# Softmax in three placed steps, reciprocals in PSUM and GpSimd's taps spread, in the first convolution of a fused convolution, Fourier and MLP kernel

## The chip, the cores and the metric

The kernel runs on one core of a Trainium2 chip. The metric is the device time of one execution in microseconds (us), as the median of three runs. Names used throughout: PE is TensorE (matmul), PEld its weight load, DVE is VectorE, ACT is ScalarE, POOL is GpSimd, SP is SyncE, whose queue issues the DMAs. SBUF is the on-chip working memory and PSUM the memory that PE writes its results to; DVE and ACT read and write both.

## The reference

There are 8 batches of 4224 positions by 192 channels, in 8 heads of 24 channels. For each batch:

```python
w = exp(weight_gen - max_k(weight_gen)); w = w / (sum_k(w) + 1e-9)     # softmax over 7 taps, by position and head
y[s, h, g] = sum_k w[s, h, k] * x_pad[s + k, h, g]                     # dynamic causal convolution, 7 taps
u = y + real(fft(fft(y, axis=positions), axis=channels))
un = (u - mean(u)) / sqrt(var(u) + 1e-6)                               # over the 192 channels
out = u + maximum(un @ w_ch1, 0) @ w_ch2                               # 192 -> 768 -> 192
```

## The kernel before

Each batch lies on 128 partitions by 33 rows of 192 channels, with halo rows in front of each half, so that a tap is a shift by one row within a partition. `conv(b)` works in chunks: chunk 8 (`NC`) is row 0 alone, and chunks 0 to 7 have four rows each, two from the lower half and their mirror images.

**Softmax.** `softmax_taps` (L261) is a generator that loads the tap weights of a batch in parts of rows, here (0, 5), (29, 33) and (5, 29), and takes each part in two steps: DMA, maximum (L273), subtraction (L274) and exponential; then sum (L278), L279 and reciprocal (L280). The result of the sum and the reciprocal is the tile `wm`, in SBUF for batch 0 and in a PSUM bank (named `wp` in the trace) for later batches. `tap_step(b, n)` drives the generator up to its n-th step. The normalised weights of a chunk are made by one multiplication (L362, for chunk 8 L365) into the PSUM tile `wp`: weights from SBUF times reciprocals.

**Taps.** For each chunk and tap DVE multiplies rows of `x_sb` by `wp` (L405). `POOL_TAPS` gives some taps of chunks 0, 1 and 3 of batch 0 to POOL, which multiplies by a copy of the weights in SBUF, `wq` (made at L374, product L403). The seven products of a chunk are added in one of two ways. For chunks 0, 1, 3, 5 and 7 of batch 0 (`PE_SUMS`) PE adds them by matmuls with the identity into two banks `pa` (L410; a product is two matmuls, each of which the trace shows as two records), and ACT copies the sum to `u` (L423). For the other chunks POOL adds them one by one (L414); in batch 1 and later DVE takes some of these. Products that PE adds are in tiles of tag `g2` with three buffers; products that POOL adds are in tag `prod` with five. The order of the taps of a chunk that PE adds is POOL's taps first, then the rest:

```python
order = [*pt, *(k for k in range(K) if k not in pt)] if pa else range(K)
```

**Groups.** In batch 0 chunks run in pairs, (8, 0), (1, 2), (3, 4), (5, 6), and then 7 alone, with the taps of a pair interleaved. After a pair come its folds on POOL (`sm`, L428 and L430), the first Fourier matmul (`pg`, L435), two copies on ACT, a sum and a difference on DVE (L444, L446), and the store of `gt` to `g_d` in DRAM. `transform(b)` reads `g_d` back and does the second Fourier step (`pp`, L481), `mix` the one over channels (`eo`, L510), `norm` the normalisation, and `mlp` the two products (`ph` L607, `po` L630).

**Order.** Every engine runs its own queue in order. The framework sets each queue's order when the kernel is built, by its own estimate of when operands are ready, starting from the order in which the code issues the work. The code orders the stages by `add`, `run`, `queue` and `behind`: `conv(0)` alone, then its transform beside the preparation of the MLP weights on DVE (`prep_w1`, `prep_w2`) and the softmax of batch 1, then the MLP of one batch beside the convolution of the next.

Of the kernel before, what the change touches and what calls it, by code (L numbers as in the profile page):

```python
# [38 lines left out]
F32_GROUPS = 7  # L39
WARM = (20, 0, 12, 12)  # L40
# [48 lines left out]
def tile_dynconv_fnet_mlp(  # L89
# [171 lines left out]
    def softmax_taps(b, parts):  # L261

        w_sb = sb.tile([P, N2 * H, K], F32, tag="w_sb", name=f"w_{b}", bufs=2)
        if b == 0:
            m = cpool.tile([P, N2 * H], F32, name=f"wm_{b}")
        else:
            m = wbanks[b][:, 4 * H * K:4 * H * K + N2 * H]
        wv = wg[b].rearrange("p r h k -> p (r h) k")
        for lo, hi in parts:
            sl = slice(lo * H, hi * H)  # L270
            n = (hi - lo) * H
            nc.sync.dma_start(w_sb[:, sl], wv[:, sl])
            nc.vector.tensor_reduce(out=m[:, sl], in_=w_sb[:, sl], axis=AX.X, op=ALU.max)  # L273
            nc.vector.tensor_tensor(out=w_sb[:, sl], in0=w_sb[:, sl],  # L274
                                    in1=m[:, sl].unsqueeze(2).broadcast_to([P, n, K]), op=ALU.subtract)
            nc.scalar.activation(w_sb[:, sl], w_sb[:, sl], AF.Exp)
            yield None
            nc.vector.tensor_reduce(out=m[:, sl], in_=w_sb[:, sl], axis=AX.X, op=ALU.add)  # L278
            nc.vector.tensor_scalar_add(out=m[:, sl], in0=m[:, sl], scalar1=1e-9)  # L279
            nc.vector.reciprocal(out=m[:, sl], in_=m[:, sl])  # L280
            yield w_sb, m
# [3 lines left out]
    def tap_step(b, n):  # L285

        t = taps[b]
        while t["n"] < n:
            t["n"] += 1
            t["tiles"] = next(t["gen"]) or t["tiles"]  # L290

# [4 lines left out]
    def conv(b):  # L296
# [22 lines left out]
        def need_taps(c):  # L319
            nonlocal w_sb, ws  # L320
            while not rows_w.issuperset(rows_of(c)):
                i = next(part_iter)
                rows_w.update(range(*parts[i]))
                tap_step(b, 2 * i + 2)
# [6 lines left out]
        if b == 0:  # L331
            need_x(NC)
            need_x(0)
            need_taps(1)
            need_x(1)
            need_taps(3)
# [3 lines left out]
        gt, tails = None, []  # L340
        for grp in groups:
            chunks = []
            wbank = wbanks[b] if b > 0 else pst("wp", 1, [P, 512], F32, f"wp_{b}_{grp[0]}")
            for i, c in enumerate(grp):
# [27 lines left out]
                elif pt:  # L372
                    wq = sb.tile([P, 2, 2 * H, len(pt)], F32, tag="wq", name=f"wq_{b}_{c}", bufs=2)
                    nc.gpsimd.tensor_tensor(out=wq, in0=win[:, :, :, pt[0]:pt[-1] + 1],  # L374
                                            in1=nin.unsqueeze(3).broadcast_to([P, 2, 2 * H, len(pt)]), op=ALU.mult)
                pa = None
                if on_pe:
                    bank = ("po", 2) if c % 4 == 3 or c == 0 == b else ("ph", 3)
                    pa = [pst(*bank, [P, 512], F32, f"pa_{b}_{c}_{i}") for i in range(2)]
                chunks.append((c, R, u, wp, pa, wq, pt))  # L380
            for i in range(K):
                for c, R, u, wp, pa, wq, pt in chunks:
                    order = [*pt, *(k for k in range(K) if k not in pt)] if pa else range(K)
# [309 lines left out]
    queue(lp, (lambda n: tap_step(1, n), 5))  # L693
# [7 lines left out]
    for g, call in ((1, (prep_w2, 2)), (1, (lambda n: tap_step(1, n), 6))):  # L701
# [82 lines left out]
```

## Time and profile before

| | |
|---|---|
| median of three runs | 1148.77 us (1147.63 to 1149.8) |
| the profiled execution | 1148.59 us, of which its span 1146.8 us |
| PE busy | 1081.0 us, 94% of the span |
| DVE busy | 979.5 us, 85% |
| POOL busy | 877.3 us, 76% |
| ACT busy | 777.8 us, 68% |
| end of the last matmul sum of `conv(0)` | 79.92 us |
| first matmul of the MLP | 125.93 us |

A row of the timeline gives the start from the beginning of the span, the length, the engine, the line and operation, the tile written and those read with their shapes, and the count of like instructions that it stands for. In brackets stand the idle time of the engine before the row and what ended it. Lines are those of the kernel before; the kernel after has the same statements up to ten lines further down. An instruction's length as recorded overlaps a little with the start of the next one on its engine: two multiplications of 128x768 on DVE start 0.87 us apart and are recorded as 0.95 us each.

### The profile page before, as it was taken

To read this page: it belongs to the slowest core of one execution; us is meant where nothing else is said; L and a number is where in the kernel's file an instruction comes from. 1 tells how busy PE (TensorE), PEld (TensorE's weight loads), DVE (VectorE), ACT (ScalarE), POOL (GpSimd) and SP (SyncE) were. 2 spreads that over 40 slices of the span, in tenths; PEclk is the share of its full clock that TensorE was granted. 3 is DMA by queue.
4 is the path that set the end of the run, shared out by engine and by line. 5 is a ranking of instruction groups with operands and counts; after the bars stand their busy time and mean duration, and the time that the engine had idled before them with its cause. 6 is when DMAs were issued, how large, how long until landed. Compare 5 with 4: busy or idle time off the path is not lost.

```text
span 1146.8 us, 23674 instructions
## 1 busy us (share of the span) xinstructions
PE 1081.0 (94%) x8476; PEld 816.4 (71%) x8476; DVE 979.5 (85%) x1825; ACT 777.8 (68%) x2360; POOL 877.3 (76%) x752
## 2 busy tenths in 40 slices
PE   5776799999899999999999999999999999999998
PEld 3345388777577877678777877778768877787777
DVE  7998998889989998999989998999989996356443
ACT  1014677455994689758985699568974898579822
POOL 5959799699996999699969999699969998011200
PEclk9998899999999999999999999999999999999999
DMA  8325244523474147514564238514651133412321
GB/s 301 127 92 155 42 103 106 182 79 80 114 206 128 36 131 196 156 46 113 133 166 110 78 104 212 132 53 118 163 138 56 57 92 92 114 44 59 84 46 46
DMA packets 156502, 128.72 MB, mean 112 GB/s; under 512 B 108571, under 2 KB 133088, under 8 KB 156384
## 3 DMA queue, kind: packets, MB, share of 16 engines
q1 hardware_dynamic: 156384, 127.21, 40.7%
q8 instruction: 67, 1.10, 0.4%
q14 instruction: 51, 0.42, 0.1%
HBM read 61.46 MB, written 39.37 MB: 88 GB/s over the span
## 4 chain that ended last, share of the span: by engine, by line
PE 54%; DVE 15%; POOL 13%; issue 8%; ACT 5%; DMA 4%; SPq 0%; DVEq 0%; POOLq 0%; ACTq 0%
PE ph L607 23%; PE po L630 20%; POOL u L414 10%; DVE pr L405 6%; PE pp L481 3%; PE eo L510 3%; PE pa L410 2%; PE pg L435 2%; DVE hh L618 2%; DMA g<-g_d 2%; POOL hl L574 1%; POOL hl L576 1%; DMA g_d<-gt 1%; ACT un L565 1%; ACT hh L617 1%
## 5 line engine op out<-in xcount | busy, mean ns | idle before, releaser
L414 POOL TENSOR_TENSOR u<-u,pr 128x768 f32<-128x768 f32 (+1 forms) x396 | 657.7, 1687 | 57.1 <-DVE pr L405 44.9
L630 PEld LDWEIGHTS <-hh 128*128 128x128 f16 x4248 | 364.6, 98 | 81.1 <-DVE hh L618 5.2
L630 PE MATMUL po<-w2h,hh 128*128 128x192 f16 x2832 | 415.1, 246 | 5.6 <-DVE hh L618 4.1
L607 PE MATMUL ph<-ht,w1h 128*128 128x512 f16 (+1 forms) x1296 | 395.3, 362 | 6.0 <-DMA ht<-hl 3.2
L405 DVE TENSOR_TENSOR pr<-x_sb,wp 128x768 f32<-128x768 f32 (+1 forms) x420 | 363.2, 888 | 16.6 <-POOL u L414 13.6
L630 PE MATMUL po<-w2l,hh 128*128 128x192 f16 x1416 | 346.4, 246 | 0.0
L618 DVE SCALAR_TENSOR_TENSOR hh<-ph,hh 128x512 f16<-128x512 f32 (+1 forms) x390 | 250.2, 647 | 107.4 <-ACT hh L617 106.6
L607 PE MATMUL ph<-ht,w1l 128*128 128x512 f16 (+1 forms) x864 | 310.4, 362 | 0.0
L617 ACT ACTIVATE hh<-ph 128x512 f16<-128x512 f32 (+1 forms) x390 | 214.1, 551 | 132.4 <-PE ph L607 105.9
L607 PEld LDWEIGHTS <-w1h 128*128 128x128 f16 x1296 | 125.7, 99 | 89.8 <-issue 0.5
L565 ACT ACTIVATE un<-u,rs 128x192 f32<-128x192 f32 x264 | 124.0, 536 | 20.8 <-POOL hl L576 9.6
L574 POOL TENSOR_TENSOR hl<-un,hl 128x512 f16<-128x512 f32 (+1 forms) x69 | 74.9, 1085 | 65.6 <-ACT hl L573 29.3
L607 PEld LDWEIGHTS <-w1l 128*128 128x128 f16 x864 | 85.2, 99 | 54.8 <-issue 7.4
L554 ACT ACTIVATE junk<-u,rs 128x192 f16<-128x192 f32 x244 | 111.0, 455 | 4.1
L550 ACT ACTIVATE junk<-u 128x192 f16<-128x192 f32 x244 | 88.4, 362 | 16.0 <-DVE u L520 13.1
L510 PE MATMUL eo<-cs_sb,pq 97*128 97x97 f32 x544 | 83.1, 276 | 3.7 <-DVE u L520 3.7
L510 PEld LDWEIGHTS eo<-cs_sb,pq 97*128 97x128 f32 x544 | 76.7, 195 | 9.6 <-issue 5.0
L485 ACT COPY pq<-pp 97x204 f32<-97x204 f32 (+1 forms) x96 | 46.9, 489 | 51.5 <-PE pp L481 51.2
L635 DVE SCALAR_TENSOR_TENSOR u<-po,isc,u 128x384 f32<-128x384 f32 (+1 forms) x122 | 74.1, 608 | 6.6 <-PE po L630 6.6
L428 POOL TENSOR_TENSOR sm<-u 128x382 f32<-128x382 f32 x64 | 66.2, 1034 | 9.0 <-ACT u L423 8.7
L410 PE MATMUL pa<-pr,ident 128*128 128x384 f32 x140 | 53.1, 519 | 20.5 <-POOL pr L403 11.3
L630 PE MATMUL po<-w2f,hh 128*128 128x192 f32 x336 | 63.0, 327 | 1.0 <-DVE u L635 1.0
(106 smaller groups left out, 1253.9 us busy)
## 6 DMA issues: line engine op xcount, KB each, us to landing
out_dram<-u SPq DMA_DIRECT2D x64, 384.0 KB
x_sb<-in_x_dram SPq DMA_DIRECT2D x48, 384.0 KB
g<-g_d SPq DMA_DIRECT2D x40, 336.0 KB
x_sb<-in_x_dram SPq DMA_DIRECT2D x8, 864.0 KB
g_d<-gt SPq DMA_DIRECT2D x32, 195.0 KB
g_d<-gt SPq DMA_DIRECT2D x32, 189.0 KB
w<-in_weight_gen_dram SPq DMA_DIRECT2D x6, 924.0 KB
x_sb<-in_x_dram SPq DMA_DIRECT2D x8, 672.0 KB
```

The source lines that it names most:

```text
L405: last_product[b] = nc.vector.tensor_tensor(out=dst, in0=rows, in1=wk, op=ALU.mult)
L410: nc.tensor.matmul(pa[h][:, 0:n], lhsT=ident32, rhs=prf[:, h * n:(h + 1) * n], start=(i == 0), stop=(i == K - 1))
L414: adder.tensor_tensor(out=u, in0=u, in1=pr, op=ALU.add)
L510: nc.tensor.matmul(eo[:, e, j, :], lhsT=pq[0:DH, e, r, r:r + P], rhs=cs_sb[:, e, :], start=True, stop=True)
L550: nc.scalar.activation(junk, uv[:, t, :], AF.Identity, accum_out=st[:, t, 0:1])
L554: nc.scalar.activation(junk, uv[:, t, :], AF.Square, bias=rs[:, 2, t:t + 1], accum_out=st[:, t, 1:2])
L565: nc.scalar.activation(halves[t // 2][:, t % 2, :], uv[:, t, :], AF.Identity, bias=rs[:, 1, t:t + 1], scale=rs[:, 0, t:t + 1])
L574: lo_eng.tensor_tensor(out=hl[:, t0:t1, 2 * P:3 * P], in0=src[:, 0:t1 - t0, 0:P], in1=hl[:, t0:t1, 0:P], op=ALU.subtract)
L607: last_ph[n] = nc.tensor.matmul(ph[:, 0:T], lhsT=wt[:, cs_], rhs=ht[:, 0:T, blk], start=(i == 0), stop=(i == len(terms) - 1))
L617: nc.scalar.activation(a[:, 0:T], ph[:, 0:T], AF.Relu)
L618: nc.vector.scalar_tensor_tensor(out=l[:, 0:T], in0=ph[:, 0:T], scalar=0.0, in1=a[:, 0:T], op0=ALU.max, op1=ALU.subtract)
L630: nc.tensor.matmul(po[t // 2][:, t % 2, :], lhsT=hx[:, t], rhs=wx[:, c2, :], start=(c2 == 0 and i == 0), stop=(c2 == NH - 1 and i == len(t ...
```

## The change

The softmax generator has three steps to a part: DMA; maximum, subtraction and exponential; sum and reciprocal. The callers' counts follow (`3 * i + 3` for `2 * i + 2`; 8 and 9 for 5 and 6), and in batch 0 the DMA of the third part is issued by itself, by `tap_step(0, 7)`, ahead of two pieces of `x`; the rest of that part is issued where chunk 2 first needs it. In batch 0 the third part's maxima, sums and reciprocals lie in a PSUM bank of tag `ph`; those of the first two parts stay in SBUF. Chunk 5 sums into the banks of chunk 1, which leaves that tag its third buffer. `wq` of chunk 3 is made by DVE. The taps of a chunk that PE adds come in the order that `TURNS` spells: `ddpdddd` for one tap of POOL, `dpddpdd` for two, where d is DVE's next tap and p is POOL's.

```diff
--- before.py
+++ after.py
@@ -37,6 +37,7 @@
 POOL_TAPS = {(0, 0): (5, 6), (0, 1): (5, 6), (0, 3): (6,), (1, 0): range(7), (1, 1): range(7)}
 DVE_ADDS = {(1, c): 1 for c in range(2, NC)}
 F32_GROUPS = 7
+TURNS = {1: 'ddpdddd', 2: 'dpddpdd', 3: 'dpddpdp'}
 WARM = (20, 0, 12, 12)
 
 
@@ -261,15 +262,18 @@
     def softmax_taps(b, parts):
 
         w_sb = sb.tile([P, N2 * H, K], F32, tag="w_sb", name=f"w_{b}", bufs=2)
-        if b == 0:
-            m = cpool.tile([P, N2 * H], F32, name=f"wm_{b}")
-        else:
+        if b > 0:
             m = wbanks[b][:, 4 * H * K:4 * H * K + N2 * H]
         wv = wg[b].rearrange("p r h k -> p (r h) k")
         for lo, hi in parts:
             sl = slice(lo * H, hi * H)
+            if b == 0 and lo == 0:
+                m = cpool.tile([P, N2 * H], F32, name=f"wm_{b}")
+            elif b == 0 and hi < N2:
+                m = pst("ph", 3, [P, 512], F32, f"wm_{b}")[:, 0:N2 * H]
             n = (hi - lo) * H
             nc.sync.dma_start(w_sb[:, sl], wv[:, sl])
+            yield None
             nc.vector.tensor_reduce(out=m[:, sl], in_=w_sb[:, sl], axis=AX.X, op=ALU.max)
             nc.vector.tensor_tensor(out=w_sb[:, sl], in0=w_sb[:, sl],
                                     in1=m[:, sl].unsqueeze(2).broadcast_to([P, n, K]), op=ALU.subtract)
@@ -289,6 +293,11 @@
             t["n"] += 1
             t["tiles"] = next(t["gen"]) or t["tiles"]
 
+    def turns(pool, turn):
+
+        its = {"p": iter(pool), "d": (k for k in range(K) if k not in pool)}
+        return [next(its[t]) for t in turn]
+
     def mirrored(ap, step):
 
         return bass.AP(ap.tensor, ap.offset, [ap.ap[0], [step, 2], *ap.ap[1:]])
@@ -321,7 +330,7 @@
             while not rows_w.issuperset(rows_of(c)):
                 i = next(part_iter)
                 rows_w.update(range(*parts[i]))
-                tap_step(b, 2 * i + 2)
+                tap_step(b, 3 * i + 3)
                 w_sb, ws = taps[b]["tiles"]
 
         if b > 0:
@@ -331,13 +340,12 @@
         if b == 0:
             need_x(NC)
             need_x(0)
-            need_taps(1)
+            tap_step(0, 7)
             need_x(1)
-            need_taps(3)
             need_x(3)
             load_consts()
         groups = [(NC, 0), (1, 2), (3, 4), (5, 6), (7,)] if b == 0 else [(c,) for c in range(NC + 1)]
-        gt, tails = None, []
+        gt, tails, sums = None, [], {}
         for grp in groups:
             chunks = []
             wbank = wbanks[b] if b > 0 else pst("wp", 1, [P, 512], F32, f"wp_{b}_{grp[0]}")
@@ -371,16 +379,18 @@
                     wq = win
                 elif pt:
                     wq = sb.tile([P, 2, 2 * H, len(pt)], F32, tag="wq", name=f"wq_{b}_{c}", bufs=2)
-                    nc.gpsimd.tensor_tensor(out=wq, in0=win[:, :, :, pt[0]:pt[-1] + 1],
-                                            in1=nin.unsqueeze(3).broadcast_to([P, 2, 2 * H, len(pt)]), op=ALU.mult)
+                    (nc.vector if c > 1 else nc.gpsimd).tensor_tensor(
+                        out=wq, in0=win[:, :, :, pt[0]:pt[-1] + 1], in1=nin.unsqueeze(3).broadcast_to([P, 2, 2 * H, len(pt)]), op=ALU.mult)
                 pa = None
                 if on_pe:
-                    bank = ("po", 2) if c % 4 == 3 or c == 0 == b else ("ph", 3)
-                    pa = [pst(*bank, [P, 512], F32, f"pa_{b}_{c}_{i}") for i in range(2)]
+                    bank = ("po", 2) if c % 4 == 3 or c == 0 else ("ph", 3)
+                    pa = sums.get(bank)
+                    if pa is None or bank[0] == "po":
+                        pa = sums[bank] = [pst(*bank, [P, 512], F32, f"pa_{b}_{c}_{i}") for i in range(2)]
                 chunks.append((c, R, u, wp, pa, wq, pt))
             for i in range(K):
                 for c, R, u, wp, pa, wq, pt in chunks:
-                    order = [*pt, *(k for k in range(K) if k not in pt)] if pa else range(K)
+                    order = turns(pt, TURNS[len(pt)]) if pt and pa else range(K)
                     k = order[i]
                     pr = u
                     if i > 0 or pa:
@@ -690,7 +700,7 @@
         if at > EARLY / N2:
             break
     queue(lp, (prep_w1, loaded[0]))
-    queue(lp, (lambda n: tap_step(1, n), 5))
+    queue(lp, (lambda n: tap_step(1, n), 8))
     for i in range(2):
         queue(lp, (prep_w2, i))
     for g in range(QUICK):
@@ -698,7 +708,7 @@
         run()
         add(0.0, 1.0, norm(0, g))
         run()
-    for g, call in ((1, (prep_w2, 2)), (1, (lambda n: tap_step(1, n), 6))):
+    for g, call in ((1, (prep_w2, 2)), (1, (lambda n: tap_step(1, n), 9))):
         queue(last_lo[g].ins, call)
 
     def rest():
```

The change moves instructions on the queues of SP, DVE and POOL at the start of batch 0. In the names below, `w_0` are the tap weights of batch 0, `pr_0_c_k` the product of chunk c and tap k, `u_0_c` a chunk's sum, `sm_0_c` its fold, `wp_0_1` the normalised weights of chunks 1 and 2.

SP's queue at the start, before:

```order
L316 DMA x_sb_66<-in_x_dram 128x1344
L316 DMA x_sb_66<-in_x_dram 128x384
L316 DMA x_sb_66<-in_x_dram 128x1728
L316 DMA x_sb_66<-in_x_dram 128x768 x2
L272 DMA w_0_91<-in_weight_gen_dram 128x1344
L316 DMA x_sb_66<-in_x_dram 128x768 x2
```

and now:

```order
L325 DMA x_sb_66<-in_x_dram 128x1344
L325 DMA x_sb_66<-in_x_dram 128x384
L325 DMA x_sb_66<-in_x_dram 128x1728
L275 DMA w_0_91<-in_weight_gen_dram 128x1344
L325 DMA x_sb_66<-in_x_dram 128x768 x4
```

The load of the third part of the weights (128x1344) stood behind two pieces of `x` (128x768) and now stands ahead of them.

DVE's queue in the first pair of chunks, before:

```order
L405 TENSOR_TENSOR u_0_8_133<-x_sb_66,wp_0_8_132 128x192
L405 TENSOR_TENSOR pr_0_8_1_146<-x_sb_66,wp_0_8_132 128x192
L405 TENSOR_TENSOR pr_0_8_2_153<-x_sb_66,wp_0_8_132 128x192
L405 TENSOR_TENSOR pr_0_0_0_156<-x_sb_66,wp_0_8_132 128x768
L405 TENSOR_TENSOR pr_0_8_3_160<-x_sb_66,wp_0_8_132 128x192
L273 TENSOR_REDUCE wm_0_92<-w_0_91 128x192
L405 TENSOR_TENSOR pr_0_0_1_163<-x_sb_66,wp_0_8_132 128x768
L405 TENSOR_TENSOR pr_0_8_4_167<-x_sb_66,wp_0_8_132 128x192
```

and now:

```order
L415 TENSOR_TENSOR u_0_8_128<-x_sb_66,wp_0_8_127 128x192
L415 TENSOR_TENSOR pr_0_0_0_137<-x_sb_66,wp_0_8_127 128x768
L415 TENSOR_TENSOR pr_0_8_1_141<-x_sb_66,wp_0_8_127 128x192
L415 TENSOR_TENSOR pr_0_8_2_148<-x_sb_66,wp_0_8_127 128x192
L415 TENSOR_TENSOR pr_0_0_1_151<-x_sb_66,wp_0_8_127 128x768
L415 TENSOR_TENSOR pr_0_8_3_155<-x_sb_66,wp_0_8_127 128x192
L277 TENSOR_REDUCE wm_0_110<-w_0_91 128x192
L415 TENSOR_TENSOR pr_0_0_2_158<-x_sb_66,wp_0_8_127 128x768
L415 TENSOR_TENSOR pr_0_8_4_162<-x_sb_66,wp_0_8_127 128x192
```

The first product of chunk 0 stands ahead of two small products of chunk 8, and two products of chunk 0 instead of one stand ahead of the maximum over the third part.

POOL's queue behind the additions of chunk 8, before:

```order
L403 TENSOR_TENSOR pr_0_1_5_221<-x_sb_66,wq_0_1_215 128x768
L403 TENSOR_TENSOR pr_0_1_6_226<-x_sb_66,wq_0_1_215 128x768
L374 TENSOR_TENSOR wq_0_3_298<-w_0_91,wm_0_92 128x32
L428 TENSOR_TENSOR sm_0_0_200<-u_0_0_135 128x2x191
L430 TENSOR_TENSOR sm_0_0_200<-u_0_0_135 128x2
L414 TENSOR_TENSOR u_0_2_219<-u_0_2_219,pr_0_2_1_230 128x768
L414 TENSOR_TENSOR u_0_2_219<-u_0_2_219,pr_0_2_2_237 128x768
```

and now:

```order
L438 TENSOR_TENSOR sm_0_0_195<-u_0_0_130 128x2x191
L440 TENSOR_TENSOR sm_0_0_195<-u_0_0_130 128x2
L413 TENSOR_TENSOR pr_0_1_5_227<-x_sb_66,wq_0_1_210 128x768
L424 TENSOR_TENSOR u_0_2_220<-u_0_2_220,pr_0_2_1_231 128x768
L413 TENSOR_TENSOR pr_0_1_6_248<-x_sb_66,wq_0_1_210 128x768
L424 TENSOR_TENSOR u_0_2_220<-u_0_2_220,pr_0_2_2_238 128x768
```

POOL's two products of chunk 1 stood ahead of the fold of chunk 0 and now stand behind it, and an addition of chunk 2 stands between the two. `wq` of chunk 3 has left this queue.

## Rows read from the trace of the kernel before

**Rows 1.** Busy time by stretch of the span, 10 to 76 us.

```profile
core 0: us, PE busy (x) PEld busy (x) DVE busy (x) ACT busy (x) POOL busy (x), PEclk, DMA share, GB/s
...
10.00:16.00 6.00, 4.67 (x8) 2.55 (x9) 3.60 (x6) 0.00 (x0) 3.29 (x3) 1.00 1.02 399
16.00:22.00 6.00, 6.00 (x20) 3.54 (x18) 6.00 (x8) 1.33 (x1) 4.32 (x4) 1.00 0.62 178
22.00:30.00 8.00, 6.66 (x22) 3.50 (x20) 7.97 (x11) 1.64 (x6) 5.23 (x7) 1.00 1.01 358
30.00:40.00 10.00, 7.76 (x22) 3.59 (x22) 9.90 (x13) 0.96 (x2) 9.84 (x8) 1.00 0.46 166
40.00:50.00 10.00, 8.55 (x27) 4.52 (x28) 10.00 (x14) 0.77 (x4) 8.87 (x7) 1.00 0.22 61
50.00:60.00 10.00, 6.82 (x25) 4.06 (x24) 9.88 (x13) 1.72 (x6) 9.06 (x9) 1.00 0.40 129
60.00:70.00 10.00, 7.49 (x21) 3.39 (x20) 9.86 (x16) 0.96 (x2) 9.24 (x6) 1.00 0.25 75
```

**Rows 2.** Timeline of DVE, 0 to 27 us: start, length, what, count, idle before.

```profile
7.38 0.61 DVE L405 TENSOR_TENSOR pr<-x_sb,wp 128x192 f32<-128x192 f32 x2
9.64 1.22 DVE L405 TENSOR_TENSOR pr<-x_sb,wp 128x768 f32<-128x768 f32 x2 [1.65 <-DMA x_sb<-in_x_dram]
13.26 1.55 DVE L273 TENSOR_REDUCE wm<-w 128x192 f32<-128x1344 f32 x1 [2.40 <-DMA w<-in_weight_gen_dram]
...
22.18 1.70 DVE L362 TENSOR_TENSOR wp<-w,wm 128x224 f32<-128x224 f32 x1
23.80 1.34 DVE L280 RECIPROCAL wm<-wm 128x192 f32<-128x192 f32 x1
...
25.83 0.95 DVE L405 TENSOR_TENSOR u<-x_sb,wp 128x768 f32<-128x768 f32 x1
```

**Rows 3.** Timeline of all engines, 0 to 60 us, two of DVE's rows.

```profile
36.85 2.93 DVE L362 TENSOR_TENSOR wp<-w,wm 128x224 f32<-128x224 f32 x2
...
52.11 2.22 DVE L362 TENSOR_TENSOR wp<-w,wm 128x224 f32<-128x224 f32 x2
```

**Rows 4.** Line 362 over the whole span: counts, then duration in ns min/median/max.

```profile
L362 DVE TENSOR_TENSOR wp<-w,wp x54: 385/396/434, 130.9 to 935.8; 128x224 f32<-128x224 f32 x54
L362 DVE TENSOR_TENSOR wp<-w,wm x8: 401/1066/1831, 6.3 to 67.7; 128x224 f32<-128x224 f32 x8
```

**Rows 5.** Timeline of POOL, 0 to 85 us.

```profile
20.64 2.98 POOL L403 TENSOR_TENSOR pr<-x_sb,wq 128x768 f32<-128x768 f32 x2 [0.24 <-PE pa L410]
...
25.64 1.00 POOL L428 TENSOR_TENSOR sm<-u 128x382 f32<-128x382 f32 x1
26.60 0.19 POOL L430 TENSOR_TENSOR sm<-u 128x2 f32<-128x2 f32 x1
27.73 7.50 POOL L414 TENSOR_TENSOR u<-u,pr 128x768 f32<-128x768 f32 x4 [0.93 <-DVE pr L405]
...
36.63 1.80 POOL L414 TENSOR_TENSOR u<-u,pr 128x768 f32<-128x768 f32 x1
...
71.83 0.21 POOL L430 TENSOR_TENSOR sm<-u 128x2 f32<-128x2 f32 x1
```

**Rows 6.** Timeline of PE, 68 to 82 us.

```profile
69.36 4.11 PE L410 MATMUL pa<-pr,ident 128*128 128x384 f32 x12 [0.95 <-DVE pr L405]
...
75.24 0.81 PE L435 MATMUL pg<-sm,f_sb 128*128 128x192 f32 x4
75.89 4.03 PE L410 MATMUL pa<-pr,ident 128*128 128x384 f32 x12
```

**Rows 7.** Timeline of PE, 120 to 132 us, the first product of the MLP.

```profile
125.93 0.38 PE L607 MATMUL ph<-ht,w1h 128*128 128x512 f16 x1
```

**Rows 8.** Busy time by stretch, 200 to 400 us: the sum over the stretches.

```profile
sum 200.00, PE 188.41 PEld 146.41 DVE 184.59 ACT 129.72 POOL 177.90; mean PE 6.28 PEld 4.88 DVE 6.15 ACT 4.32 POOL 5.93
```

**Rows 9.** PE's waits, 130 to 400 us: who for whom, total, times, longest.

```profile
PE po L630 <- DVE hh L618: 3.4, 1, 3.4
```

## Prediction

> **What bounds the kernel now.** The page shows PE busy for most of the span, but the change touches only the first 80 us, before the MLP begins, so I read that part on its own. First the busy time by stretch [rows 1]: from 30 to 70 us DVE is busy 9.86 to 10.0 of every 10 us, POOL 8.87 to 9.84, PE 6.8 to 8.6. So DVE bounds the first convolution, POOL runs close behind, and PE follows. Then DVE's timeline, for what its time is spent on that is not work [rows 2]. It waits 1.65 us for the first large piece of `x`, and 2.40 us, until 13.26, for the third part of the tap weights, which stands in the DMA queue behind two pieces of `x`. From there on it has no wait worth counting until the last chunk. Then the instructions that are longer than they need be: the product that makes the normalised weights, line 362. It takes 1.70 us at 22.18, 2.93 us for two at 36.85 and 2.22 us for two at 52.11 [rows 2, 3], while the same instruction with the reciprocals in PSUM takes 385 to 434 ns in all 54 cases of the later batches, and 401 ns in the best case with both inputs in SBUF [rows 4]. POOL's timeline shows what the long ones lie beside: two products from 20.64 to 23.62, and an addition from 36.63 to 38.43 [rows 5]. As these rows read, a DVE product with both inputs in SBUF stands still while POOL works there.
>
> What follows is a chain. The last matmul sum of this convolution ends at 79.92 (75.89 and 4.03) [rows 6]; fold, transform, mixing and normalisation hang on it, and the first MLP matmul starts at 125.93 [rows 7]. The inputs that come from outside (weights, tables, the next batch) are loaded long before, so I expect a gain at 80 us to arrive at the end.
>
> **The load moved ahead.** The 128x1344 load no longer waits for two pieces of 128x768 in 4 bytes, 786 KB. At the 399 GB/s of the stretch from 10 to 16 us [rows 1] that is 1.97 us, so the weights land at 11.3 instead of 13.26. DVE now starts at 9.64 with a product of chunk 0 (0.87), two small ones (0.27 each; before, they ran at 7.38 in a wait [rows 2]), a second product of chunk 0 (0.87) and a small one (0.27), and reaches the maximum at 12.19. Nothing is left to wait for. Before, the maximum started at 13.26 with that second product still to do: 13.26 + 0.87 - 12.19 = **1.94 us** gained. If the load came no sooner, the maximum would start at 13.26 and 0.87 would be left; that is the lower end.
>
> **Taps spread.** PE now starts after DVE's first product at 10.5 instead of POOL's at 11.3, and gets POOL's products between DVE's. At first a matmul record takes 0.58 us (8 in 4.67), later 0.30 (20 in 6.00) [rows 1], with the same granted clock beside both; four records make a product. PE adds the first three in about 6.5 us, until 17.1. The fourth product of DVE needs the buffer of the third sum, and DVE is ready at 16.54, after the second large softmax instruction: **-0.56 us** (0 to -1). Chunk 0 is complete on PE at about 22.7. POOL's products of chunk 1 now stand behind the fold of chunk 0, so POOL is idle from 19 to about 23.9, and DVE's product for chunk 1, whose reciprocals stay in SBUF, runs without a neighbour at 20.9: 1.62 us from start to next start [rows 2] become 0.42, **1.2 us** (between 0, should POOL run there after all, and 1.3).
>
> **Reciprocals in PSUM.** Chunks 2 to 7 read them from there. The two pairs take 2 x 0.396 instead of 2.93 and 2.22 [rows 3, 4]: 2.14 and 1.43. DVE takes over `wq` of chunk 3, 128x32; I put it at 0.2, the order of the smallest products it does. Together **3.37 us** (2.9 to 3.5). The sums and reciprocals themselves I cost at nothing: DVE's cost does not change with the memory, to judge by line 362 (396 against 401 ns uncontended [rows 4]).
>
> [...]
>
> **Sum on DVE**: 1.94 - 0.56 + 1.2 + 3.37 = 5.95 us by the time DVE starts chunk 7.
>
> **What is late next: POOL.** From the fold of chunk 0, done at about 25.1, POOL has 18 additions at 1.87 (7.50 for four), 3 products at 1.45, and 6 folds at 1.15 (1.00 and 0.19) [rows 5]: 44.9 us, to 70.0, against 72.04 now. PE needs the last of these folds between products of chunk 7. Now it takes it at 75.24 and has three products (12 records, 4.03 us) behind it [rows 6], so POOL has 3.2 us to spare. After the change chunk 7 starts at 63.4 (69.36 less 5.95) and PE wants that fold after five products and one earlier `pg`, at about 70.5, with two products behind it. The slack shrinks to 0.5 us. DVE, POOL and PE then finish almost together, and three queues that tight lose something to each other: **-0.5 us** (0 to -2.5, the last if POOL idles 3 us as it does now, see below). Gain at the end of the convolution: 5.45 us, 3.4 with that last end, 6.7 with all the upper ends; all the lower ends together would leave 0.3.
>
> **Behind it** DVE prepares weights without pause and PE, ACT and DMA follow; all start by the convolution's end, and move with it. The order of the queues differs in places in the MLP of batches 0 and 1 and the start of batch 2, a few instructions swapped with neighbours; I count that as 0, plus or minus 1.
>
> The profiled execution took 1148.59 us, 0.18 below the median of the runs shown. 1148.59 - 5.45 = 1143.1; against the median **1143.3 us**.
>
> **Rivals.**
> *POOL sets the end.* From 30 to 70 us POOL is idle 3.0 of 40 us [rows 1], mostly for DVE's products (0.93 before 27.73 [rows 5]). If it idles as long in the new order it ends at 73.0, three us late, 2.5 more than the slack; the gain is 5.95 - 2.5 = 3.4, the time 1145.3. Against it: DVE runs ahead of POOL by more than before, so there is less to wait for. 14%.
> *The contention stays.* If line 362 is slow for another reason, such as the tile it writes, 3.37 falls away and the gain is 2.1 to 2.6: 1146.4. Against it stand the 54 rows. 4%.
> *The gain is given back.* Between 200 and 400 us PE is idle for 200 - 188.4 = 11.6 us [rows 8]. If those waits hang on something that does not move, such as loads that are paced by buffers, PE waits longer and the gain goes: about 1148, no change. I see no such resource, but 270 us of other work lie between. 12%.
> *Slower: the new order on PE in the MLP of batches 0 and 1.* PE takes its queue in order. Its longest wait there is 3.4 us for DVE's low halves `hh` [rows 9]. Matmuls have changed places by a block of five or ten, and one put ahead of its operand holds all behind it. From 5.45 us more idle time the gain is gone; at 7.8 the kernel is slower by 0.2%. If the idle time doubled the result would be 1143.3 + 11.6 = 1154.9. For it: these queues are set by estimates that the change has shifted. Against: few rows moved, and PE has MLP work either side. 8%.
>
> **Chances.** 0.2% (2.3 us) is about what a measurement of this kernel can tell from no change. The forecast, 1141.8 to 1144.8, has 62%. With the first two rivals the kernel is faster by over 0.2% in 80%, within it in 12%, slower in 8%. The range runs from 1141.5 (a gain of 6.7 and some luck in the order) to 1147.2, which leaves out the slower case, the upper half of the third rival, and little below.
>
> **What would show it.** In the changed profile: the wait before the maximum of the third part under 0.3 us; the products for chunks 2 to 7 near 0.4 us each, the one for chunk 1 too; PE's first sum at about 10.5 and the fold of chunk 0 on POOL at about 24; the last fold of POOL before chunk 7's near 70; the last sum of the convolution ending at 74 to 75 and the first MLP matmul at 120 to 121. The prediction is wrong in its first half if the convolution ends after 77, and in its second if the first MLP matmul comes 5 us sooner and the end does not.

## The result and the profile after

| | before | after |
|---|---|---|
| time, median (us) | 1149.8 (5 runs, 1147.63 to 1154.99) | 1141.5 (5 runs, 1139.6 to 1143.36) |
| profiled execution, span (us) | 1146.8 | 1139.7 |
| last matmul sum of the first convolution ends | 79.92 | 73.88 |
| first MLP matmul starts | 125.93 | 118.64 |

The ratio of the times is 0.9935, 95% interval 0.9915 to 0.9955. The change makes the kernel faster by 0.65%; the forecast was 1143.3 us, with a range of 1141.5 to 1147.2. The measured median thus lies at the lower end of the range, outside the 1141.8 to 1144.8 that had 62%: by the ratio the whole gained 7.5 us, where 5.45 was forecast.

DVE's timeline in the changed kernel, 5 to 72 us, the counterpart of [rows 2, 3] (start, length, what, count, idle before and what ended it; its lines stand 4 to 10 lower than before's):

```profile
9.14 2.61 DVE L415 TENSOR_TENSOR pr<-x_sb,wp 128x768 f32<-128x768 f32 x5 [2.12 <-DMA x_sb<-in_x_dram]
11.67 1.55 DVE L277 TENSOR_REDUCE wm<-w 128x192 f32<-128x1344 f32 x1
...
16.89 1.22 DVE L415 TENSOR_TENSOR pr<-x_sb,wp 128x768 f32<-128x768 f32 x2 [0.76 <-PE pa L420]
...
20.61 0.39 DVE L370 TENSOR_TENSOR wp<-w,wm 128x224 f32<-128x224 f32 x1
20.91 1.36 DVE L284 RECIPROCAL wm<-wm 128x192 f32<-128x192 f32 x1
...
33.99 0.40 DVE L370 TENSOR_TENSOR wp<-w,wm 128x224 f32<-128x224 f32 x1
34.30 0.20 DVE L382 TENSOR_TENSOR wq<-w,wm 128x32 f32<-128x32 f32 x1
34.42 0.40 DVE L370 TENSOR_TENSOR wp<-w,wm 128x224 f32<-128x224 f32 x1
35.41 0.95 DVE L415 TENSOR_TENSOR pr<-x_sb,wp 128x768 f32<-128x768 f32 x1 [0.59 <-DVE wp L370]
...
47.71 0.82 DVE L370 TENSOR_TENSOR wp<-w,wm 128x224 f32<-128x224 f32 x2
...
62.21 3.62 DVE L415 TENSOR_TENSOR pr<-x_sb,wp 128x768 f32<-128x768 f32 x4
```

The maximum of the third part starts at 11.67 without a wait, where it started at 13.26 after 2.40 of waiting. The weight products of chunks 1 to 7 are short. Over the whole span (count, then duration in ns min/median/max), the 54 of later batches and the eight of batch 0, which took 401/1066/1831 before [rows 4]:

```profile
L370 DVE TENSOR_TENSOR wp<-w,wp x54: 369/382/397, 123.9 to 928.8; 128x224 f32<-128x224 f32 x54
L370 DVE TENSOR_TENSOR wp<-w,wm x8: 383/393/400, 6.2 to 61.7; 128x224 f32<-128x224 f32 x8
```

POOL's timeline, 5 to 80 us, the folds of chunk 0 and of the last chunk before 7 [rows 5]:

```profile
22.93 0.99 POOL L438 TENSOR_TENSOR sm<-u 128x382 f32<-128x382 f32 x1 [4.09 <-ACT u L433]
...
67.47 0.99 POOL L438 TENSOR_TENSOR sm<-u 128x382 f32<-128x382 f32 x1
68.42 0.20 POOL L440 TENSOR_TENSOR sm<-u 128x2 f32<-128x2 f32 x1
```

PE's timeline, 5 to 76 us, and further on at the first MLP matmul, where [rows 6, 7] were read:

```profile
10.24 10.47 PE L420 MATMUL pa<-pr,ident 128*128 128x384 f32 x24 [10.24 <-DVE pr L415]
...
63.31 4.11 PE L420 MATMUL pa<-pr,ident 128*128 128x384 f32 x12 [1.29 <-DVE pr L415]
...
70.49 0.81 PE L445 MATMUL pg<-sm,f_sb 128*128 128x192 f32 x4
71.14 2.74 PE L420 MATMUL pa<-pr,ident 128*128 128x384 f32 x8
...
118.64 0.39 PE L617 MATMUL ph<-ht,w1h 128*128 128x512 f16 x1 [0.27 <-DMA ht<-hl]
```

The gain grows along the convolution. The first pair of weight products starts 2.86 us sooner than in [rows 3] (33.99 for 36.85), the second 4.40 (47.71 for 52.11), chunk 7's block of twelve matmul records 6.05 (63.31 for 69.36, [rows 6]), and the last sum ends 6.04 sooner. The first MLP matmul gains 1.25 more, 7.29. On DVE the sum `gt` of chunk 7 stood at 84.08 before and stands at 77.20 now, 6.88 sooner: in the new order it stands ahead of two instructions of the weight preparation (`pw_w` and `pa_w`) that it stood behind.

### The profile page after: what moved, and what is told of

It reads as the page before. It is cut to its first block, busy times and chain, and to the rows that moved or that the text cites. A ratio compares the mean times of both kernels' runs of the same rounds, so it can differ in the third digit from the quotient of the medians.

```text
span 1139.7 us, 23676 instructions
## 1 busy us (share of the span) xinstructions
PE 1078.6 (95%) x8476; PEld 818.6 (72%) x8476; DVE 975.2 (86%) x1826; ACT 776.2 (68%) x2360; POOL 874.7 (77%) x751
## 4 chain that ended last, share of the span: by engine, by line
PE 54%; POOL 12%; DVE 12%; issue 10%; ACT 5%; DMA 4%; SPq 0%; DVEq 0%; POOLq 0%; ACTq 0%
PE ph L617 23%; PE po L640 21%; POOL u L424 9%; PE pp L491 4%; DVE pr L415 3%; PE eo L520 3%; PE pg L445 2%; DMA g<-g_d 2%; DVE hh L628 1%; DMA g_d<-gt 1%; ACT un L575 1%; POOL sm L438 1%; ACT hh L627 1%; PE pa L420 1%; POOL hl L586 1%
## 5 line engine op out<-in xcount | busy, mean ns | idle before, releaser
L415 DVE TENSOR_TENSOR pr<-x_sb,wp 128x768 f32<-128x768 f32 (+1 forms) x420 | 359.0, 875 | 18.6 <-POOL u L424 13.9
L628 DVE SCALAR_TENSOR_TENSOR hh<-ph,hh 128x512 f16<-128x512 f32 (+1 forms) x390 | 245.2, 633 | 105.1 <-ACT hh L627 104.2
L575 ACT ACTIVATE un<-u,rs 128x192 f32<-128x192 f32 x264 | 124.1, 535 | 24.2 <-POOL hl L586 10.9
```

Of the source, the lines that this page charges most:

```text
L415: last_product[b] = nc.vector.tensor_tensor(out=dst, in0=rows, in1=wk, op=ALU.mult)
L575: nc.scalar.activation(halves[t // 2][:, t % 2, :], uv[:, t, :], AF.Identity, bias=rs[:, 1, t:t + 1], scale=rs[:, 0, t:t + 1])
L628: nc.vector.scalar_tensor_tensor(out=l[:, 0:T], in0=ph[:, 0:T], scalar=0.0, in1=a[:, 0:T], op0=ALU.max, op1=ALU.subtract)
```

## The experiments

Twelve runs follow, each timed beside the kernel before on the same chip (its medians there were 1149.0, 1149.62 and 1150.12). "Sum ends" is the end of the last matmul sum of the first convolution, "MLP" the start of the first MLP matmul, both from the profiled execution. The last column counts PE's matmul rows, from the program's end backwards, that stand in the same order as in the changed kernel, which has 13443; it is counted in the built programs. The trace shows 8476 matmul records, and the same count in it gives 5890 where the column has 10126, 1797 for 3275, and 1215 to 1532 for 2332 to 2787.

| run | sum ends | MLP | time, median | ratio to before (95%) | rows in the same order |
|---|---|---|---|---|---|
| before | 79.92 | 125.93 | 1149.8 | 1 | 10126 |
| after | 73.88 | 118.64 | 1141.5 | 0.9935 (0.9915 to 0.9955) | all |
| e1 reciprocals in SBUF | 76.75 | 122.55 | 1147.74 | 0.9990 (0.9965 to 1.0015) | 10126 |
| e2 POOL's taps first | 76.57 | 122.04 | 1150.74 | 1.0014 (1.0001 to 1.0026) | 2787 |
| e3 load late | 75.93 | 122.68 | 1153.18 | 1.0035 (1.0007 to 1.0062) | 2337 |
| e4 PSUM alone | 76.52 | 122.61 | 1147.22 | 0.9979 (0.9963 to 0.9995) | 10126 |
| e5 load alone | 76.54 | 124.00 | 1154.02 | 1.0039 (1.0022 to 1.0055) | 2332 |
| e6 taps alone | 81.14 | 127.19 | 1149.55 | 1.0003 (0.9989 to 1.0017) | 2332 |
| e7 chunk 8 first | 72.95 | 120.20 | 1149.36 | 0.9995 (0.9981 to 1.0008) | 2777 |
| e8 28 early matmuls | 72.58 | 119.95 | 1145.41 | 0.9967 (0.9949 to 0.9984) | 2787 |
| e9 after again | 74.21 | 118.11 | 1143.41 | 0.9937 (0.9913 to 0.9962) | all |
| e10 8 early matmuls | 73.63 | 120.00 | 1142.73 | 0.9933 (0.9909 to 0.9957) | all |
| e11 12 early matmuls | 73.89 | 121.00 | 1146.96 | 0.9969 (0.9955 to 0.9984) | 3275 |
| e12 e2 and 16 early matmuls | 76.70 | 121.46 | 1150.97 | 1.0004 (0.9987 to 1.0021) | 10126 |

### One part undone (e1, e2, e3)

**e1** puts the third part's reciprocals back into SBUF:

```diff
-            elif b == 0 and hi < N2:
-                m = pst("ph", 3, [P, 512], F32, f"wm_{b}")[:, 0:N2 * H]
```

> The changed kernel with the reciprocals of the third part back in SBUF, everything else kept. Theory (PSUM frees DVE from POOL, worth 3.4 of the 6.0 us gained at the end of the first convolution): the two pairs of weight products for chunks 3 to 6 are long again wherever POOL works beside them, 1.1 to 1.8 us each instead of 0.39; the last sum of the convolution ends at 76.5 to 77.5 instead of 73.9, the whole takes about 1144.5. Rival (the memory of the reciprocals does not matter, the order of the queues does): 0.4 us each, end of the sums at 74, the time stays at 1141.5.

The sum ends 2.87 us later than with the change. DVE's timeline, 30 to 56 us, has one of the two pairs long again:

```profile
34.90 2.74 DVE L368 TENSOR_TENSOR wp<-w,wm 128x224 f32<-128x224 f32 x2
...
50.54 0.82 DVE L368 TENSOR_TENSOR wp<-w,wm 128x224 f32<-128x224 f32 x2
```

The two products of the first pair took 0.83 and 1.88; the second pair, in the same memory, is as short as in PSUM. POOL's timeline of e1, 44 to 56 us, shows it idle beside that pair, from 50.37 to 51.44:

```profile
51.44 0.99 POOL L436 TENSOR_TENSOR sm<-u 128x382 f32<-128x382 f32 x1 [1.07 <-DVE wp L368]
```

So it is not the memory alone that makes them long: with POOL idle beside them, two took 0.82 from SBUF. One more instruction is longer in e1, which neither the prediction nor the theory counted: the subtraction of the third part's maxima, beside POOL in both kernels. DVE's timelines, 12 to 20 us, of e1 and then of the changed kernel:

```profile
15.15 1.96 DVE L276 TENSOR_TENSOR w<-w,wm 128x1344 f32<-128x1344 f32 x1
```

```profile
14.58 1.54 DVE L278 TENSOR_TENSOR w<-w,wm 128x1344 f32<-128x1344 f32 x1
```

The time of the whole kernel, 1147.74 where 1144.5 was expected, is 6.2 us above the changed kernel's: 3.4 more than the convolution accounts for.

**e2** gives a chunk POOL's taps first again:

```diff
-TURNS = {1: 'ddpdddd', 2: 'dpddpdd', 3: 'dpddpdp'}
+TURNS = {1: 'pdddddd', 2: 'ppddddd', 3: 'pppdddd'}
```

> The changed kernel with POOL's taps first again in each chunk that PE adds. Theory (the spread taps are worth little by themselves: 1.2 us at the weight product of chunk 1, less a wait of 0.6 to 0.8 us of DVE for PE): the weight product of chunk 1 is long again, 1 to 1.7 us, PE's first sum starts after POOL's product at about 10.8; the end of the sums moves from 73.9 to 74.4 to 75, the whole by less than 1 us. Rival (the spread carries the gain): end of the sums after 76, the whole 3 us longer.

The sum ends 2.69 us later, as the rival had it (after 76), and the loss is not where the theory had put it: the weight product of chunk 1, expected to be long, took 0.40. Up to chunk 2 this variant is even ahead (DVE's first product of chunk 2 at 23.03, in the changed kernel at 23.84). It falls back at chunk 3. PE's timeline, 5 to 78 us:

```profile
39.26 5.83 PE L420 MATMUL pa<-pr,ident 128*128 128x384 f32 x12 [4.50 <-POOL pr L413]
```

PE's sum of chunk 3 waits 4.50 us for POOL's one product, which stands behind six additions (11.29 us from 26.48); its twelve records then take 5.83 us, at a granted clock of 0.72 from 40 to 46 us. In the changed kernel that sum starts at 36.51 with DVE's products. The kernel before had no such wait either: its product on POOL stood behind four additions, and PE took up chunk 3 behind DVE. POOL's and PE's rows of the kernel before:

```profile
35.19 1.48 POOL L403 TENSOR_TENSOR pr<-x_sb,wq 128x768 f32<-128x768 f32 x1
...
41.69 1.56 PE L410 MATMUL pa<-pr,ident 128*128 128x384 f32 x4 [0.89 <-DVE pr L405]
```

In e2 DVE then waits 2.20, by my reading for a free buffer (the row names POOL's fold):

```profile
41.52 1.82 DVE L415 TENSOR_TENSOR pr<-x_sb,wp 128x768 f32<-128x768 f32 x2 [2.20 <-POOL sm L440]
```

**e3** issues the load of the third part behind the two pieces of `x` again:

```diff
-            tap_step(0, 7)
             need_x(1)
+            tap_step(0, 7)
```

> The changed kernel with the load of the third part of the weights behind two pieces of x again. Theory (the earlier load is worth 1.9 us on DVE): DVE waits 1 to 1.5 us before the maximum of the third part, which starts near 13.0 instead of 11.7; the end of the sums moves from 73.9 to 75 to 76, the whole to about 1143. Rival (the wait only moves to where DVE waits for PE, 0.76 us now, and POOL sets the end anyway): end of the sums at 74.2 or less.

The sum ends 2.05 us later; the maximum starts at 15.71 for 11.67, since DVE now does three products ahead of it that wait 1.43 for PE. The time is 11.7 us up, where 1.5 was expected.

### One part alone (e4, e5, e6)

**e4** is the changed kernel with the edits of e2 and e3, so the reciprocals in PSUM alone.

> The changed kernel with both undone, POOL's taps first and the load behind two pieces of x: the reciprocals in PSUM and the three steps remain. Theory: against the kernel before, the pairs of weight products are worth 3.4 us, so the end of the sums comes at 76 to 77 and the whole is 3 to 4 us shorter than before. Rival (the parts are worth nothing alone, only together): end of the sums at 79 or later.

**e5** is the kernel before with the three steps and the early load:

```diff
             nc.sync.dma_start(w_sb[:, sl], wv[:, sl])
+            yield None
...
-                tap_step(b, 2 * i + 2)
+                tap_step(b, 3 * i + 3)
...
-            need_taps(1)
+            tap_step(0, 7)
             need_x(1)
-            need_taps(3)
...
```

> The kernel before with one part of the change alone: three steps and the load of the third part ahead of two pieces of x. Theory: DVE's wait of 2.40 us before that maximum falls below 0.3, about 1.9 us come off the end of the sums (79.9 to about 78), the whole about 2 us shorter; the long weight products stay. Rival (POOL or PE takes the time over at once): the end of the sums stays at 79.5 to 80.

**e6** is the kernel before with `turns` and `TURNS` and nothing else.

> The kernel before with the spread of POOL's taps alone. Theory: worth between -0.6 and +1.2 us at the end of the sums, the weight product of chunk 1 short if POOL's products of chunk 1 stand behind the fold of chunk 0; the whole within 1.5 us of the kernel before. Rival (the spread is what lets DVE and PE run): 3 us or more.

At the end of the sum PSUM alone gains 3.40 us, the load alone 3.38 and the taps alone lose 1.22; together they gain 6.04. The load's 3.38 is more than the forecast's 1.94 because the weight product of chunk 1 is then short too. DVE's timeline of e5, 5 to 40 us:

```profile
22.05 0.83 DVE L362 TENSOR_TENSOR wp<-w,wm 128x224 f32<-128x224 f32 x2
...
34.13 2.33 DVE L362 TENSOR_TENSOR wp<-w,wm 128x224 f32<-128x224 f32 x2
```

POOL works there: one of its products ends at 22.17 and the next long one starts at 22.53. The long pair at 34.13 is still there.

e6's loss lies outside the -0.6 to +1.2 that was expected, and it comes at the very end, with TensorE's clock. In e6 the weight product of chunk 1 is short (0.38 at 21.91) without the early load, but the subtraction takes 2.58 beside POOL. Its last sum still starts 0.48 us sooner than before's (69.36 [rows 6]); then its first twelve records take 5.80 instead of 4.11. PE's row, and the busy time by stretch (the column behind POOL's is the granted clock of TensorE):

```profile
68.88 5.80 PE L416 MATMUL pa<-pr,ident 128*128 128x384 f32 x12 [2.02 <-DVE pr L411]
```

```profile
40.00:46.00 6.00, 6.00 (x10) 3.27 (x11) 5.54 (x7) 0.00 (x0) 6.00 (x6) 0.50 0.13 33
70.00:74.00 4.00, 4.00 (x9) 2.22 (x8) 2.08 (x3) 0.00 (x0) 3.37 (x5) 0.58 0.49 196
```

The kernel before and the changed kernel have 1.00 in both stretches. So what the taps' order is worth alone is not cleanly shown; on top of the other two parts it is worth 2.69.

The times do not follow. e5 gains 3.4 us in the convolution and the kernel is 4.4 us slower than before, where 2 us faster was expected; e4 keeps 2.4 of an expected 3 to 4.

### More early gain (e7, e8)

**e7** issues all of chunk 8's taps before chunk 0's; **e8** puts 28 small matmuls ahead of PE's first sum, which has little else to do there:

```diff
+            passes = [[(i, q) for q in chunks] for i in range(K)]
+            if b == 0 and grp[0] == NC:
+                passes = [[(i, q) for i in range(K)] for q in chunks]
...
```

```diff
+        if b == 0:
+            keep_warm(("fft", 2), "start", ident32, ident32, 28)
```

> The changed kernel with all seven taps of chunk 8 issued ahead of chunk 0, so that DVE does six small products in the 2.1 us in which it waits for x. Theory (DVE's time counts to the end of the convolution): six products of 0.27 us leave the path, 1.3 to 1.6 us; the end of the sums comes at 72.3 to 72.6, the whole at about 1140. Rival (POOL, with 45 us of work behind the fold of chunk 0 and now 0.4 us of slack, sets the end): the end of the sums at 73.5 or later.

> The changed kernel with 28 matmuls of the identity with itself on PE ahead of the first product, whose results nobody reads. Theory (PE's slow first eight records make DVE wait 0.76 us and hold up the fold of chunk 0): the records of the first sum take 0.33 us from the first on, chunk 0 is complete 2 to 2.6 us earlier (ACT's copy at about 19.5 instead of 21.7, since DVE's last product of chunk 0 then sets it, not PE), DVE does not wait for PE, POOL's fold of chunk 0 starts at about 20.7 instead of 22.9; the end of the sums gains 0.7 us, DVE's share. Rival (POOL sets the end): the gain there is 2 us.

Both end the convolution sooner than the changed kernel, by 0.93 and 1.30 us: e7 less than its theory's 1.3 to 1.6, e8 between its theory's 0.7 and the rival's 2. In e8 the first twelve records of PE's sum take 4.04 us, where 24 took 10.47 in the changed kernel. PE's timeline of e8, 5 to 26 us:

```profile
4.61 6.06 PE L470 MATMUL warm_start<-ident 128*128 128x128 f32 x43
10.51 4.04 PE L422 MATMUL pa<-pr,ident 128*128 128x384 f32 x12
```

The granted clock reads 1.00 beside the slow first records too [rows 1], so that column does not tell why they are slow. And both kernels are slower than the changed one, e7 by as much as the whole change gained, where 1140 was expected.

### What happens behind the convolution (e9 to e12)

The runs that lost most, e2, e3, e5 and e7, and e8 too, have one thing in common: the framework had set another order behind the convolution, to within some 2300 to 2800 matmul rows of the end. So it had in e6, which did not lose. The edits shift its estimates, and a few small matmuls at the start are enough to change them. With 8 of them the queues of PE, DVE, ACT and POOL keep the changed kernel's order row for row; with 12 they do not. So the order could be tried alone.

> The changed kernel once more, with its order untouched, beside the three below. Theory (the order that the scheduler gives the engines behind the first convolution decides how much of the early gain reaches the end; the changed kernel has the order of before in the last 10126 of its 13443 matmul rows): the gain of the first convolution arrives, 1140 to 1143.5 us, 6 to 9 us under before. Rival (the 1141.5 us were a lucky draw of transfer times, as its few short waits at 722 and 848 us suggest): 1145 to 1148 us, as the variants without one part of the change gave.

> The changed kernel with 8 small matmuls on the identity ahead of the first convolution's first sum; every engine's order behind them is the changed kernel's row for row. Theory (order decides): 1140 to 1143 us, no more than 1 us from the changed kernel; the 28 matmuls of the earlier run, whose order differed in some 4400 matmul rows, cost 4 us by that order. Rival (the early matmuls themselves, by the clock that they raise or the start that they hold up, cost what the earlier run lost): 1144 to 1146 us.

> The same with 12 instead of 8 of these matmuls: four more instructions of about 0.2 us each on an engine that is idle there, but the scheduler gives another order behind them (1900 of the rows at 11 of 13 thousand and 1770 at 16 move by hundreds of places in the list; the last 3275 rows are the same). Theory (order decides): slower than with 8 by 2 to 6 us, 1143.5 to 1148 us, while the first convolution ends within 0.6 us of the other. Rival (order is worth nothing): within 1 us of the run with 8.

The gain recurs (e9), and the pair e10, e11 differs by four small matmuls and the order: their sums end at 73.63 and 73.89, their first MLP matmul 1.0 us apart, and their times 4.2 us apart, with intervals that do not reach the other's median; no execution of e10 took over 1144.94 us, none of e11 under 1145.17. Two places show how. PE's waits in e10, then e11, 466 to 480 us (who for whom, total, times, longest):

```profile
PE pp L493 <- DMA g<-g_d: 0.8, 1, 0.8
```

```profile
PE pp L493 <- DMA g<-g_d: 3.5, 1, 3.5
```

and the busy time by stretch, e10 and then e11:

```profile
400.00:410.00 10.00, 8.31 (x71) 6.18 (x69) 9.41 (x20) 8.71 (x31) 10.00 (x11) 1.00 0.82 246
475.00:485.00 10.00, 10.00 (x95) 8.10 (x94) 9.88 (x15) 6.83 (x17) 9.79 (x7) 1.00 0.45 134
```

```profile
400.00:410.00 10.00, 6.71 (x26) 3.90 (x25) 9.17 (x20) 9.58 (x36) 10.00 (x12) 0.67 0.91 258
475.00:485.00 10.00, 9.21 (x57) 6.94 (x58) 7.10 (x11) 4.74 (x13) 9.61 (x6) 0.66 0.67 147
```

Where a batch's `transform` begins, PE waits for the load of `g`, which DVE's `gt` sets off. In e11's order that load comes 2.7 us later beside PE, and right behind the wait TensorE runs part of the stretch at the lower of its two levels. The granted clock stands at 1.00 or at 0.50 in the traces of the kernels before and after (0.50 from 293 to 296 us before and from 203.1 to 206.4 after), and in e11 two `ph` matmuls start 0.42 us apart behind this wait (at 478.62) where they start 0.22 apart ahead of it (at 461.03). At a mean of 0.66 the clock costs up to 3.4 of 10 us (10 x 0.34), an estimate for an engine that is busy throughout. At 403 us it is a wait of 2.3 us for DVE's `rs`, with 0.67 behind it. By the transform at 605 us e11 is 8.0 us behind e10, and 3.4 of that comes back later.

**e12** was to show that e2 loses only its 2.7 us once the late order is that of the changed kernel (its last 10126 rows; 16 early matmuls bring it about).

> GpSimd's taps first in each chunk, as in the earlier run at 1150.7 us, with 16 of the small matmuls ahead, by which the scheduler gives the last 10126 matmul rows the order of before and of the changed kernel again. Theory (order decides): the first convolution ends at 76 to 77 us, 2.7 us later than in the changed kernel, and that alone is lost: 1143.5 to 1146.5 us. Rival (taps first cost GpSimd's time later too, whatever the order): 1149 to 1151.5 us, as in the earlier run.

It did not: 1150.97, as e2. The theory falls in this form. Its sum ends at 76.70 and PE waits 2.93 for POOL's product at 40.58, as e2 did. In the profiled executions 2.8 us of the 7.4 by which it is slower than the changed kernel are lost by the first MLP matmul, and 4.6 later, with PE's rows in the same order: at `transform` PE waits 1.9 us at 475, and the clock drops there and again at 853:

```profile
475.00:485.00 10.00, 7.87 (x61) 6.29 (x62) 7.19 (x12) 5.03 (x14) 7.49 (x5) 0.83 0.73 168
853.00:863.00 10.00, 9.24 (x70) 7.33 (x71) 9.29 (x13) 5.68 (x15) 9.51 (x6) 0.83 0.73 138
```

What differs is the time that the store of `gt` and the load of `g` take. e1 shows it most plainly, since around this place every instruction stands as in the changed kernel (its profiled execution took 1153.52 us, well above the median of 1147.74). SP's queue in e1, 719 to 727 us, and in the changed kernel, 714 to 722:

```profile
720.40 1.19 SPq L458 DMA_DIRECT2D g_d<-gt  x1
724.73 1.38 SPq L479 DMA_DIRECT2D g<-g_d  x3
```

```profile
715.40 0.87 SPq L460 DMA_DIRECT2D g_d<-gt  x1
718.41 1.38 SPq L481 DMA_DIRECT2D g<-g_d  x3
```

From the last store's issue to the load's issue it is 4.33 against 3.01 us. PE waits 3.2 us for `g` in e1, 1.6 in the changed kernel. Busy time behind the wait, e1 and then the changed kernel:

```profile
725.00:735.00 10.00, 6.80 (x46) 4.60 (x45) 8.24 (x12) 3.23 (x8) 8.28 (x5) 0.83 0.75 177
```

```profile
720.00:730.00 10.00, 8.37 (x77) 6.54 (x75) 9.96 (x14) 5.56 (x15) 8.25 (x5) 1.00 0.78 181
```

**What the time behind the convolution is made of.** Add up, in each profiled execution, PE's idle time and the time at the lower level of its clock from the first MLP matmul to the end (us):

| run | whole | PE idle | lower clock | whole less idle, less half the lower clock |
|---|---|---|---|---|
| before | 1020.9 | 23.4 | 7.4 | 993.8 |
| after | 1021.1 | 24.2 | 6.8 | 993.4 |
| e10 | 1020.7 | 25.3 | 3.7 | 993.5 |
| e11 | 1024.4 | 24.1 | 13.7 | 993.5 |
| e12 | 1025.6 | 25.2 | 13.7 | 993.6 |
| e3 | 1026.8 | 29.1 | 7.0 | 994.2 |

The last column is nearly the same in all fourteen (991.7 to 994.2), so the two terms account for nearly all of what the runs lost there. e11 does not idle longer than e10: it lost by the clock alone. e12 lost 1.0 by waits and 3.5 by the clock, with the late order kept. e3 lost by waits, and not by the clock; they are waits for `ht`, and not for `g`. PE's waits for it from the first MLP matmul on, e3 and then the changed kernel:

```profile
PE ph L617 <- DMA ht<-hl: 10.5, 9, 3.9
```

```profile
PE ph L617 <- DMA ht<-hl: 3.3, 3, 1.6
```

The other executions of the pair agree: the granted clock over the span is 0.984 to 0.988 in all six of e10 and 0.979 to 0.981 in all twelve of e11.

Why the transfers of e12 are slower, with PE's order kept, is open; none of its twelve executions took under 1148.2 us, but only the profiled one shows its transfers. PE's and DVE's queues differ from the changed kernel's only in their first 25 and 40%, and it was not tried further.

## Why the prediction held, and where it did not

**The forecast came true**: 1143.3 us against 1141.5 and, repeated, 1143.41. The gain at the convolution's end was 6.04 against 5.45. That the two are so close is in part luck, since errors in the parts cancel.

**The load moved ahead.** Forecast 1.94, and 2.05 when undone (e3). The maximum started at 11.67 for 12.19, because DVE's first large product also started 0.5 us sooner (9.14 for 9.64).

**Taps spread.** The wait for PE came at the forecast place, 0.76 for 0.56. (The prediction's 6.5 us for PE's first three products is not what the record times beside it give, 8 x 0.58 + 4 x 0.30 = 5.8, by which DVE would not wait at all. The trace bears the 6.5 out: twelve records took 6.44, since the slow ones start 0.64 apart.) The step that failed is the size of this part, which rested on the weight product of chunk 1. That product is short, as forecast (0.39 at 20.61). The spread does that without the early load (0.38 in e6, 0.39 in e3), but so does the early load without the spread (0.40 in e5 and e2); only without both is it long (1.40 in e4). So undoing the taps alone could not cost the 1.2 us. Their worth, 2.69 us with the rest of the change in place, lies at chunk 3, where in e2 PE waits for a product of POOL that stands behind six additions (4.50 us; 2.94 in e4). The kernel before did not have that wait, so there the spread averts a loss that the rest of the change brings. I looked at POOL's place in the queue for chunk 1 and not for chunk 3. The forecast's 0.64 for this part was too little, but since parts overlap (undone one by one they cost 2.87, 2.69 and 2.05, 7.61 together) the sum came out near.

**Reciprocals in PSUM.** 3.37 forecast, 2.87 when undone, 3.40 alone. The products of chunks 2 to 7 took 383 to 396 ns as forecast. Not forecast was the wait of 0.59 us before 35.41. The row names the weight product just made, which had ended by then; e3 has 0.62 at the same place and names PE, so what DVE waits for is open. Nor did the sum have the subtraction of the maxima, which took 1.54 to 1.56 us in every run with the maxima in PSUM, and 1.79 to 2.58 in e1, e5 and e6 (1.55 in the kernel before, where it began ahead of POOL's addition).

That the sums and reciprocals cost nothing more in PSUM nearly came out: the sum over 128x1344 takes 1.55 us with its result in PSUM (at 18.02) and 1.55 in SBUF before (at 19.58), and the reciprocal of 128x192 1.36 in PSUM for 1.34 in SBUF [rows 2]. The instruction between them takes 0.36 in PSUM (at 20.34), as it did before in SBUF beside POOL (at 21.90), and 0.25 in SBUF in e5 (at 18.57, ahead of POOL's start at 18.79). Weight products with one input in PSUM take 383 to 396 ns, those from SBUF alone 391 and 400.

**POOL late next.** Forecast 0.5 us lost and POOL's last fold at 70.0. The fold ended at 68.62, PE wanted it at 70.49, 1.9 us to spare instead of 0.5, and nothing was lost: the gain was 6.05 at the start of chunk 7's sum and 6.04 at its end. Of the rival in which POOL sets the end nothing was seen.

**Behind it, "0, plus or minus 1".** This is where the prediction was right without a good reason. Here the order came out well: 1.25 us more by the first MLP matmul, and the rest arrives. Of the seven runs with another order behind the convolution, six end 2.5 to 8 us worse than their gain there would give, and e6 0.9 better (worked out as the gain of the sum against 1 less the ratio, times 1149). That is the outcome of the rival "slower through the new order", and 8% was far too little for it. Its mechanism, more idle time on PE, holds for e3 and in part for e5 and e7 (29.1, 26.9 and 27.9 us idle behind the first MLP matmul, for 24.2 in the changed kernel); in e2, e8 and e11 PE idles 22.5 to 24.8, and what they lost is the lower clock, which the prediction did not consider. I judged it by the number of rows that had moved, and the change had indeed kept before's order in 10126 of 13443; but the bound of 1 us was no reading of the trace. The runs show what a place in it is worth: a wait of 2 to 3.5 us for `g`, part of which PE would have idled elsewhere, and up to 3.4 through the clock behind it.

**The gain is given back** (12%) did not happen here. It did happen in part in e1 and wholly in e12, through longer waits for `g` and, for the most part, through the lower clock behind them (24.1 and 13.7 us of it behind the first MLP matmul, for 6.8 in the changed kernel).

## What to carry to other kernels

When one edit shifts a scheduler's estimates, compare the queues' orders to the very end of the program before the gain is summed, price the places where the pacing engine waits for a transfer, and add up its idle time and its time at the lower clock: here these two explained what no count of moved rows did. Test an edit's own worth at a mark right behind it (here the end of the convolution) and not by the total, and try another order that costs nothing before a good edit is thrown away: four small matmuls on an idle engine moved this kernel by 4.2 us. When products of two engines are added in turn, look at how long the slower engine's queue is at each chunk.

## What the runs showed of the hardware

- POOL does not slow DVE's product from SBUF throughout. The ones that began while a POOL instruction ran lasted until some 0.25 us behind its end (22.18 to 23.88 beside POOL's 20.64 to 23.62, 36.85 to 38.68 beside 36.63 to 38.43 [rows 2 to 5]); those of e2 and e5 that began at 21.77 and 22.05, about 0.1 us before a POOL product ended, took 0.40. The subtraction of 128x1344, both inputs in SBUF and 1.55 us by itself, ended 1.41 to 1.42 us behind the end of the POOL instruction that it began beside, in e1 (17.12 for 15.70), e5 (14.58 for 13.17) and e6 (18.53 for 17.12).
- In these rows the instruction that started first went on. In the kernel before, the other way round, the subtraction began at 15.86 and took its 1.55; POOL's addition of 128x192 began at 16.08 beside it and took 1.78 instead of 0.59.
- PE's waits for `g` of 2.8 to 3.5 us in e1, e2, e7 and e11 were each followed by a stretch at the lower clock: the mean granted clock was 0.83 in e1 (3.2 us of waiting; 725 to 735 us), and 0.66 in e2 (2.8; 728 to 733), e7 (3.0; 858 to 868) and e11 (3.5; 475 to 485). Shorter ones are not told apart by their length: 1.6 to 2.1 us were followed by a granted clock of 1.00 in the changed kernel, e9 and e10 (near 720 and 846 us), 1.8 us in the kernel before (728 to 733) and 2.2 us in e3 (at 485) too, and 1.9 us at 475 in e12 by 0.83.
